# Attention, routed experts and a SoLU layer: another order in attention and at its two ends, and a shorter way to the first expert

## The chip, the cores and the metric

One core of a Trainium2 chip runs the whole program. The time is device microseconds (us) for one execution; smaller is better. Three timed runs of the kernel before gave 783.28, 784.56 and 783.23 us, median 783.28.

## The reference

Three stages in float32, each on the output of the one before.

- Attention in chunks, 4 batches, 8 heads, 768 positions, head size 64. Each chunk of 32 queries sees 8 memory keys, 16 keys to its left, its own 32 and 8 to its right: `a = exp(s - max(s)); a / (sum(a) + 1e-9); out = a @ v`.
- A mixture of experts over 3072 tokens of 512, 8 experts, 1024 hidden. `logits = x @ w_gate`; all 3072 * 8 pairs are taken from the largest logit down, each token goes to the first expert that still has room, and an expert holds 384 tokens. Then `relu(x @ w1[e]) @ w2[e]` for the tokens of expert e.
- A SoLU layer: `h = x @ w_in`, `h * softmax(h)`, a layer norm over 1024 with scale g, and `@ w_out`.

## The kernel before

Two rows and columns of float32r stand for one float32 number: a tile is split in a rounded high part (`..h`, made by ScalarE) and the rest (`..l`, made by VectorE), and a product is three matmuls, high*high, low*high, high*low. So each weight and each activation needs a conversion before TensorE can use it.

**Attention** (`attention`) goes over 24 tiles of 128 queries (NT = 24). Iteration i of one loop works on several tiles: sums(i-1), score(i), less(i) (subtract the maximum), trans(i-2) (transpose the probabilities), expo(i), pv(i-3) (times V), xtrans(i-4) (transpose the result for the gate), and the gate's matmuls every four tiles. Five more iterations drain the pipeline. k is read into block-diagonal tiles KD (5 buffers) and v into VD (4 buffers), whose zeros are set once, by VectorE and GpSimd in turn; the loads of k, q and v are issued on SP's queue, five tiles ahead for k and q. The last four tiles' logits come from `gate_last`, eight matmuls each. The matmul results lie in four kinds of PSUM banks of two buffers each, s, t, o and, for the probabilities' transposes, those of x and the gate's, t again.

**Conversions.** w_in and w_out come as 64-bit numbers. A chunk of 512 columns (`Fixed.chunk`) is loaded on SP's queue, then goes through a step of ScalarE, four of VectorE (in the rows: `e<-v`, `v<-v,e`, `e<-v`, `e<-raw,e`), one of ScalarE and one or two of GpSimd. Seven of w_in's eight chunks are put beside attention, w_out's beside the first two experts.

**The order** of instructions on every engine is written out when the program is built. `Pace` holds a small model of each engine's clock; a generator that says `yield "spare", "dve"` gets its next step only when the model has that engine free before the next due time of more urgent jobs, less a margin `fit` (FIT in the router's first search, and in attention as well, FIT_OUT later). `limit` is the highest rank of job that may go on.

**Routing** (`Route.rounds`): for each expert in turn a search over thresholds (eight comparisons, each counted by TensorE) finds the cut; then prefix sums give each chosen token a slot, and `compact` turns slots into a list of 384 token numbers with one-hot matmuls. It carries a token number as column number and row number in bfloat16, since these keep whole numbers up to 256 only. For expert 0 nothing else can run; from expert 1 on it runs beside TensorE's matmuls.

**Experts** (`Experts.run`): when expert 0 is known its weights are loaded by indirect DMAs on GpSimd's queue, when its tokens are known x is gathered (`gather`), transposed (`x_prep`) and split; then `g12` does the first and second matrix in eight slices, `g3` w_in, `soft` the SoLU, `g4` w_out. `load_w` loads slices of both matrices, `split_w` makes a job that waits for the slice, copies it on ScalarE and subtracts on VectorE.

## Time and profile before

| | |
|---|---|
| median of three runs | 783.28 us |
| profiled execution | 785.33 us |
| its span | 783.6 us |
| TensorE busy (PE) | 715.6 us, 91% |
| VectorE busy (DVE) | 528.2 us, 67% |
| ScalarE busy (ACT) | 335.9 us, 43% |
| GpSimd busy (POOL) | 199.2 us, 25% |
| granted TensorE clock, mean | 0.962 |

The span is the time from the first to the last record; the profiled execution's own time is a little longer. Busy shares are means over stages that differ, so the stages have to be read apart: attention up to about 119 us, the search for expert 0 up to about 145, the first expert up to about 206, and then the stretch in which TensorE hardly stops. Nearly all instructions carry the same line (398), that of the helper which passes them to the model, so groups are told apart by their tiles: `s` scores, `mx` maximum, `p` probabilities, `t` and `pt` their transposes, `o` the product with v, `xs`, `xt` the result and its transposes, `g` the gate, `h` and `y` the first and second matrix of an expert.

### The profile page before, as it was taken

How to read it: one execution, taken by the hardware profiler on the slowest of the kernel's cores; microseconds unless marked ns; L12 is line 12 of the kernel's file. 1: busy time of each engine (PE TensorE's matmuls, PEld its weight loads, DVE VectorE, ACT ScalarE, POOL GpSimd, SP SyncE). 2: the span in 40 equal slices, each digit the busy share in tenths (PEclk: the TensorE clock that was granted, in tenths of full speed). 3: DMA queues.
4: the chain of work that ended last, by engine and by line, in shares of the span. 5: the costliest groups of instructions: out<-in, count | busy, mean ns of one | idle time of the engine just before them, and what ended most of it. 6: DMA issues, size and time to landing. Idle time of an engine off the chain costs nothing.

```text
span 783.6 us, 14636 instructions
## 1 busy us (share of the span) xinstructions
PE 715.6 (91%) x5760; PEld 616.5 (79%) x5760; DVE 528.2 (67%) x1434; ACT 335.9 (43%) x646; POOL 199.2 (25%) x263
## 2 busy tenths in 40 slices
PE   6988784499989999999999999999999999999993
PEld 5766674378869978988898789888988898899882
DVE  7788866589997986972897289639964852553150
ACT  1565550234374354432742273237324632563170
POOL 5234530432441134004101420232023211410121
PEclk8999995689999999999999999999999999999997
DMA  7999873532360044004400430152015110600100
GB/s 252 343 323 331 320 286 132 202 103 60 110 227 1 1 162 131 5 1 147 150 1 17 160 120 1 36 181 81 1 55 188 55 40 28 220 10 1 40 14 27
DMA packets 30020, 89.35 MB, mean 114 GB/s; under 512 B 4224, under 2 KB 4352, under 8 KB 29952
## 3 DMA queue, kind: packets, MB, share of 16 engines
q0 software_dynamic: 13056, 46.14, 17.3%
q1 hardware_dynamic: 16896, 42.28, 15.6%
q8 instruction: 45, 0.74, 0.4%
q14 instruction: 23, 0.19, 0.1%
HBM read 75.83 MB, written 12.58 MB: 113 GB/s over the span
## 4 chain that ended last, share of the span: by engine, by line
PE 72%; DVE 17%; issue 3%; ACT 3%; DMA 2%; POOL 1%; POOLq 0%; DVEq 0%; ACTq 0%
PE h L398 32%; PE y L398 16%; PE o L398 15%; PE tp L398 4%; PE r L398 3%; DVE e L398 3%; DVE sum L398 2%; DMA xg<-x_dram,idx 2%; DVE p L398 2%; DVE mx L398 1%; DVE ge L398 1%; ACT p L398 1%; DVE w1l L398 1%; PE xtp L398 1%; PE g L398 1%
## 5 line engine op out<-in xcount | busy, mean ns | idle before, releaser
L398 PE MATMUL y<-hh,w2h 128*128 128x384 f32 x256 | 91.6, 358 | 7.9 <-DVE e L398 7.9
L398 PE MATMUL y<-hl,w2h 128*128 128x384 f32 x256 | 88.3, 345 | 0.0
L398 PE MATMUL y<-hh,w2l 128*128 128x384 f32 x256 | 87.1, 340 | 0.0
L398 POOL DMA_INDIRECT raw<-in_w_dram,iw x64 | 62.3, 974 | 81.7 <-DVE w1l L398 29.8
L398 POOL DMA_INDIRECT out_dram<-ob,idx x24 | 24.3, 1014 | 227.4 <-ACT ob L398 227.0
L398 DVE TENSOR_REDUCE nm<-h 128x1 f32<-128x512 f32 x48 | 33.0, 687 | 72.6 <-PE h L398 72.3
L398 PE MATMUL o<-out_h,lh 128*128 128x512 f32 x192 | 77.2, 402 | 0.0
L398 PE MATMUL h<-in_h,yh 128*128 128x512 f32 x192 | 76.5, 399 | 0.0
L398 PE MATMUL h<-in_l,yh 128*128 128x512 f32 x192 | 76.2, 397 | 0.0
L398 PE MATMUL h<-in_h,yl 128*128 128x512 f32 x192 | 75.9, 396 | 0.0
L398 PE MATMUL o<-out_h,ll 128*128 128x512 f32 x192 | 75.6, 394 | 0.0
L398 PE MATMUL o<-out_l,lh 128*128 128x512 f32 x192 | 75.1, 391 | 0.0
L398 ACT ACTIVATE hh<-h 128x384 fp32r<-128x384 f32 x64 | 31.4, 491 | 90.4 <-PE h L398 77.3
L398 PE MATMUL h<-xh,w1l 128*128 128x384 f32 x256 | 60.1, 352 | 2.5 <-DVE w1l L398 2.4
L398 PE MATMUL h<-xh,w1h 128*128 128x384 f32 x256 | 59.5, 349 | 1.2 <-ACT w1h L398 1.2
L398 ACT CAST w2h<-raw 128x512 fp32r<-128x512 f32 x64 | 39.6, 620 | 48.0 <-PE y L398 43.5
L398 PE MATMUL h<-xl,w1h 128*128 128x384 f32 x256 | 58.1, 346 | 0.0
L398 PEld LDWEIGHTS y<-hh,w2h 128*128 128x128 f32 x256 | 48.2, 188 | 9.8 <-DVE e L398 9.6
L398 DVE TENSOR_TENSOR xl<-tp,xh 128x512 fp32r<-128x512 f32 x24 | 16.6, 690 | 50.2 <-ACT xh L398 35.2
L398 DVE TENSOR_TENSOR w2l<-raw,w2h 128x512 fp32r<-128x512 f32 x64 | 43.8, 685 | 8.7 <-ACT w2h L398 8.7
L398 PEld LDWEIGHTS h<-xh,w1l 128*128 128x128 f32 x256 | 46.6, 195 | 3.3 <-DVE w1l L398 3.2
L398 PEld LDWEIGHTS y<-hl,w2h 128*128 128x128 f32 x256 | 48.5, 189 | 0.2
(194 smaller groups left out, 1603.1 us busy)
## 6 DMA issues: line engine op xcount, KB each, us to landing
vd<-in_vx_dram SPq DMA_DIRECT2D x48, 256.0 KB, 5.3
kd<-in_kx_dram SPq DMA_DIRECT2D x48, 176.0 KB, 5.0
qt<-in_q_dram SPq DMA_DIRECT2D x24, 256.0 KB, 4.9
x_dram<-xs SPq DMA_DIRECT2D x6, 1024.0 KB, 9.8
raw<-in_win_dram SPq DMA_DIRECT2D x8, 512.0 KB, 6.0
raw<-in_wout_dram SPq DMA_DIRECT2D x8, 512.0 KB, 3.7
raw<-in_w_dram,iw POOLq DMA_INDIRECT x64
xg<-x_dram,idx POOLq DMA_INDIRECT x24
```

What stands on the lines that cost most here:

```text
L398: return fn(*args, **kw)
```

## The change

- Attention: q of a tile is loaded ahead of k. The clears are shared among VectorE, ScalarE and GpSimd in another order. The 20 warm-up transposes go. The router's constants become a job of the model that takes spare steps. In an iteration, score and less come first, then sums of the tile before, then P times V, and only then the exponential; the transposes of the probabilities go to the end. The transposes of x get banks of their own.
- The end of attention: no new conversion steps in the last two tiles and the drain (limit 0); three of the last four tiles' logits go through the short form of the gate, in spare banks of the scores.
- FIT and FIT_OUT are larger.
- Compaction carries a token number as one float16 number between -1536 and 1535; the slot gets 32 added, so that it also says whether a token is chosen.
- First expert: only one slice of w1 is loaded before the gather of x, the others behind it. The first slice is split at once. Small float16 matmuls are issued before and between the transposes of x. The router's round 1 begins when x is ready (`hold`).

```diff
-FIT = 0.34
-FIT_OUT = 0.27
+FIT = 0.62
+FIT_OUT = 0.5
...
 def warm(nc, p, a, n):
     for i in range(n):
-        nc.tensor.transpose(p[:, i % 4], ident, ident)
+        nc.tensor.matmul(p[:, i % 4], a, a, start=True, stop=True)
...
         def load_kq(i):
             if i < NT:
+                nc.sync.dma_start(QT[i % AHEAD], q[i])
                 for h2 in range(2):
                     nc.sync.dma_start(KD[i % AHEAD][h2::2, h2], kx[i, h2])
-                nc.sync.dma_start(QT[i % AHEAD], q[i])
...
-        for i in range(AHEAD):
-            (nc.gpsimd if i % 2 else nc.vector).memset(KD[i], 0.0)
-            if i < AHEAD - 1:
-                (nc.vector if i % 2 else nc.gpsimd).memset(VD[i], 0.0)
+        def clear(t):
+            flat = ...
+            nc.scalar.activation(flat, zero.to_broadcast([128, flat.shape[1]]), AF.Copy)
+        nc.vector.memset(KD[0], 0.0)
+        clear(KD[1])
+        nc.gpsimd.memset(KD[2], 0.0)
+        nc.vector.memset(VD[0], 0.0)
+        clear(KD[3])
+        nc.gpsimd.memset(VD[1], 0.0)
+        clear(VD[2])
+        nc.gpsimd.memset(KD[4], 0.0)
+        nc.gpsimd.memset(VD[3], 0.0)
...
-        consts()
-        warm(nc, ps.tile([128, 4, 128], F32, tag="t", name="warm"), ident, 20)
+        pace.add(consts(), FIRST_C, 0)
...
         for i in range(NT + 5):
+            if i == NT - 2:
+                pace.limit = 0
+            if i < NT:
+                s = score(i)
+                less(i, s)
+                load_kq(i + AHEAD)
             n = 0
             for _ in sums(i - 1) if 0 <= i - 1 < NT else ():
                 beside(i, n)
                 n += 1
-            if i < NT:
-                s = score(i)
-                less(i, s)
-                load_kq(i + AHEAD)
-            if 0 <= i - 2 < NT:
+            if i >= NT and i - 2 < NT:
                 trans(i - 2)
-            if i < NT:
-                expo(i)
             beside(i, 3)
             if 0 <= i - 3 < NT:
                 pv(i - 3)
+            if i < NT:
+                expo(i)
...
-            if i > NT:
-                gate_last(i - 5)
+            if NT < i < NT + 4:
+                gate(NT // 4 - 1, (i - NT - 1,), 2)
+            if i == NT + 4:
+                gate_t(NT // 4 - 1, 3)
+                gate_last(NT - 1)
             if NT + 1 >= i >= 6 and (i - 6) % 4 == 3:
                 gate_t((i - 6) // 4)
+            if 2 <= i < NT:
+                trans(i - 2)
...
-            V.tensor_tensor(slot, slot, sf, op=ALU.mult)
+            V.scalar_tensor_tensor(slot, slot, 32.0, sf, op0=ALU.add, op1=ALU.mult)
             yield 0.0
-            s1 = self.t("s1", [NT])
-            V.tensor_tensor(s1, sel[:, 0], sel[:, 1], op=ALU.add)
...
-        V.scalar_tensor_tensor(am, sl, 32.0, low, op0=ALU.add, op1=ALU.subtract)
-        V.tensor_tensor(am, am, s1, op=ALU.mult)
+        V.tensor_tensor(am, sl, low, op=ALU.subtract)
...
-        V.tensor_tensor(rhs[:, :, 0], rhs[:, :, 1], self.cnum[:, :, None].to_broadcast([128, NT, A]), op=ALU.mult)
-        yield idle
-        V.tensor_scalar(rhs[:, :, 1], rhs[:, :, 1], self.col, None, op0=ALU.mult)
+        V.tensor_tensor(rhs, rhs, self.tok[:, :, None].to_broadcast([128, NT, A]), op=ALU.mult)
...
-        tok = self.t("tok", [TT])
-        V.tensor_scalar(tok, p[:, 0:TT], 128.0, None, op0=ALU.mult)
         idx = self.k.tile([128, TT], I32, name=f"idx{r}")
-        V.tensor_tensor(idx, tok, p[:, TT:2 * TT], op=ALU.add)
+        V.tensor_scalar(idx, p[:, 0:TT], float(N // 2), None, op0=ALU.add)
...
-        self.load_w(0, range(2))
+        self.load_w(0, (0,), (1,))
...
         self.gather(0)
-        self.load_w(0, (2,))
+        self.load_w(0, (0,), (2,))
+        self.load_w(0, (1, 2))
         self.fixed.hold = False
-        for f in range(2):
-            self.split_w(0, f, (1,))
+        self.split_w(0, 0, (1,), True)
+        p = self.ph.tile([128, 4, 128], F32, tag="h", name="warm")
+        warm(nc, p, self.route.ones, 40)
+        for t in range(TT):
+            self.x_prep(0, t)
+            warm(nc, p, self.route.ones, 5)
+        self.split_w(0, 1, (1,))
         for f in range(2):
             self.split_w(0, f, (2,))
-        warm(nc, self.ph.tile([128, 4, 128], F32, tag="h", name="warm"), self.ident, 25)
-        for t in range(TT):
-            self.x_prep(0, t)
         for t in range(TT):
             self.need("x", 0, t)
+        self.route.hold = False
```

## Rows read from the trace of the kernel before

**Rows 1.** Windows: stretch, its length, busy us of each engine, granted clock, DMA share, GB/s.
```profile
12.00:105.00 93.00, 76.62 (x1660) 58.64 (x1664) 74.71 (x150) 52.86 (x101) 39.29 (x34) 0.94 0.90 314
105.00:118.70 13.70, 12.43 (x211) 10.42 (x201) 7.46 (x18) 6.27 (x13) 2.54 (x2) 1.00 1.03 384
...
145.00:153.40 8.40, 5.81 (x38) 4.88 (x36) 1.95 (x4) 2.33 (x5) 4.75 (x5) 0.86 0.84 282
153.40:165.40 12.00, 9.59 (x75) 7.70 (x75) 8.47 (x26) 3.66 (x8) 2.41 (x2) 0.57 0.34 115
165.40:206.00 40.60, 37.99 (x350) 33.44 (x349) 38.95 (x100) 16.31 (x30) 11.06 (x8) 1.00 0.20 58
...
287.00:783.60 496.60, 478.69 (x2710) 419.10 (x2708) 296.28 (x836) 210.89 (x408) 101.58 (x162) 0.99 0.21 70
```

**Rows 2.** Groups of VectorE, 12 to 105 us: count, busy us, mean ns, idle before.
```profile
L398 DVE TENSOR_TENSOR p<-s,mx 128x512 f32<-128x512 f32 x23 | 16.0, 696 | 2.6 <-POOL p L398 0.5
L398 DVE TENSOR_REDUCE sum<-p 128x8 f32<-128x512 f32 x23 | 15.9, 693 | 10.9 <-ACT p L398 10.7
L398 DVE TENSOR_REDUCE mx<-s 128x8 f32<-128x512 f32 x23 | 15.2, 662 | 1.0 <-PE s L398 0.8
L398 DVE TENSOR_SCALAR e<-v 128x512 int32<-128x512 int32 x12 | 8.0, 675 | 0.1
L398 DVE SCALAR_TENSOR_TENSOR v<-v,e 128x512 int32<-128x512 int32 x6 | 5.8, 974 | 0.1
L398 DVE TENSOR_SCALAR sum<-sum 128x8 f32<-128x8 f32 x23 | 5.4, 234 | 0.8
L398 DVE SCALAR_TENSOR_TENSOR e<-raw,e 128x512 f32<-128x512 uint32 x6 | 4.8, 800 | 0.1
L398 DVE RECIPROCAL rec<-sum 128x8 f32<-128x8 f32 x23 | 4.7, 202 | 0.8
```

**Rows 3.** Timeline, attention's first and last maximum: start us, length, engine, what.
```profile
6.78 1.93 PE L398 MATMUL s<-kd,qt 128*32 128x128 f32 x32 [0.88 <-DMA qt<-in_q_dram]
...
9.49 0.13 DVE L398 TENSOR_SCALAR tri<-row,col 128x128 f16<-128x128 bf16 x1
...
11.51 0.06 DVE L398 MEMSET power<- 128x3 f32 x1
...
11.78 0.69 DVE L398 TENSOR_REDUCE mx<-s 128x8 f32<-128x512 f32 x1
...
105.15 0.69 DVE L398 TENSOR_REDUCE mx<-s 128x8 f32<-128x512 f32 x1
```

**Rows 4.** Timeline, TensorE: the scores of two tiles that follow each other.
```profile
21.64 1.05 PE L398 MATMUL s<-kd,qt 128*32 128x128 f32 x32
...
24.80 1.08 PE L398 MATMUL s<-kd,qt 128*32 128x128 f32 x32
```

**Rows 5.** Windows of 2 us in attention's first tiles, for the granted clock.
```profile
18.00:20.00 2.00, 1.88 (x29) 1.39 (x20) 1.42 (x3) 0.56 (x2) 1.04 (x1) 0.50 1.02 381
...
22.00:24.00 2.00, 2.00 (x61) 1.63 (x52) 1.30 (x2) 1.27 (x3) 0.47 (x1) 1.00 1.01 373
```

**Rows 6.** Timeline of the drain: the last tile's probabilities and their product.
```profile
110.66 0.59 ACT L398 COPY pt<-t 128x512 f32<-128x512 f32 x1 [0.35 <-PE t L398]
...
113.48 1.08 PE L398 MATMUL o<-vd,pt 128*32 128x128 f32 x32
```

**Rows 7.** Timeline from expert 0's compaction to its first matmuls.
```profile
141.48 0.29 DVE L398 TENSOR_SCALAR rhs<-rhs,col 128x288 bf16<-128x288 bf16 x1
...
144.68 0.16 DVE L398 TENSOR_SCALAR tok<-r 128x3 f32<-128x3 f32 x1 [0.30 <-PE r L398]
...
145.30 0.95 POOL L398 DMA_INDIRECT xg<-x_dram,idx  x1 [1.78 <-DVE idx L398]
...
149.45 0.66 PE L398 MATMUL tp<-ident,xg 128*128 128x128 f32 x4 [0.58 <-DMA xg<-x_dram,idx]
...
156.81 0.69 PE L398 MATMUL h<-xh,w1l 128*128 128x384 f32 x1 [2.41 <-DVE w1l L398]
```

More of the change, by code (lines that the diff above doesn't have):

```diff
@@ L177, in attention, with spare, gate @@
         G = {}
-        def gate(u, js=range(4)):
+        def spare():
+            return ps.tile([128, 4, 128], F32, tag="s", name="sp")
+        def gate(u, js=range(4), last=3):
             if js[0] == 0:
-                G[u] = ps.tile([128, 128], F32, tag="t", name="g")
+                G[u] = spare()[:, 0] if last < 3 else ps.tile([128, 128], F32, tag="t", name="g")
             for kc in range(4):
@@ L186, in gate @@
                                      skip_group_check=True)
[L187 removed]
+            if js[-1] == last:
+                n = 32 * last + 32
                 g, G[u] = G[u], wk.tile([128, 128], F32, tag="gs", name="gs", bufs=2)
[L189 removed]
+                nc.scalar.copy(G[u][0:n], g[0:n])
         def gate_last(i):
[L193 removed]
+            g = spare()[:, 0, 0:E]
             for kc in range(4):
@@ L531, in __init__ @@
         self.idx, self.iw = {}, {}
-        self.held, self.stage = False, 0
+        self.held, self.stage, self.making, self.hold = False, 0, True, True
     def consts(self, ident):
@@ L750, in rounds @@
             if r:
-                yield from self.compact(r, s1, sl)
+                yield from self.compact(r, sl)
             else:
-                self.beside.add(self.compact(r, s1, sl))
-                while r not in self.idx:
+                self.beside.add(self.compact(r, sl))
+                while r not in self.idx or self.hold:
                     yield 0.0
@@ L862, in load_w, with split_w, parts @@
                 self.W[r, n, qq] = t
-    def split_w(self, r, f, ns=(1, 2)):
+    def split_w(self, r, f, ns=(1, 2), now=False):
         nc = self.nc
-        def parts(n):
+        def parts(n, now=False):
             raw = self.W[r, n, f // 2][:, f % 2]
@@ L870, in parts @@
             lo = self.ws.tile([128, 512], F32R, tag=f"l{n}", name=f"w{n}l")
-            yield raw
+            if not now:
+                yield raw
             nc.scalar.copy(h, raw)
-            yield "act"
+            if not now:
+                yield "act"
             nc.vector.tensor_tensor(lo, raw, h.bitcast(F32), op=ALU.subtract)
@@ L876, in split_w @@
         for n in ns:
-            self.beside.add(parts(n), 0, 0)
+            if now:
+                for _ in parts(n, now):
+                    pass
+            else:
+                self.beside.add(parts(n), 0, 0)
     def gather(self, r):
@@ L1207, in step @@
         beside.tick()
-    attention(nc, tc, q, kx, vx, wg, ident, x_dram, L, lambda: route.consts(ident), step)
+    attention(nc, tc, q, kx, vx, wg, ident, x_dram, L, lambda: route.consts(ident), beside, step)
+    while route.making:
+        beside.tick()
+    beside.limit = 9
     route.open_psum(ctx)
```

63 lines of the change are left out of this document (38 added, 25 removed).

## The prediction

> **What bounds the kernel now.** I read the share of each engine first, then the stretches, then, for each stretch that the change touches, the groups of instructions with the idle time in front of them. The program has two parts. From 287 us on TensorE is busy for 478.69 of 496.60 us at a granted clock of 0.99 [rows 1]: nothing in the change removes TensorE work there, so I count no gain or loss in it. Before that no engine is full, and the time is set by order. In the attention loop (12 to 105 us) VectorE is busy 74.71 us of 93, TensorE 76.62, and the DMA engines 0.90 of the time [rows 1]. The reader is to see in the groups of VectorE that the largest single idle time has one cause: 10.7 us in front of the row sums, released by ScalarE's exponential [rows 2]. The old order issues the exponential of tile i right behind its subtraction and then wants its sum next, so VectorE stands still. A tile takes (105.15 - 11.78) / 23 = 4.06 us [rows 3]. In the drain (105 to 118.7) the engines are a serial chain; the search for expert 0 runs to 145 and is a chain too; then the first expert starts slowly: clock 0.57 from 153.4 to 165.4, and VectorE busy 38.95 of the next 40.60 us [rows 1].
>
> **The sum is made against the profiled execution,** 785.33 us, of which 783.60 are the span and 1.73 lie around it. The median of the three timed runs is 783.28, so 2.05 us come off at the end.
>
> **Attention's start.** Now the scores of tile 0 end at 6.78 + 1.93 = 8.7 us, but their maximum starts at 11.78, since VectorE is first in clears and then, from 9.49 to 11.57, in the router's constants [rows 3]. The change gives VectorE two clears instead of five, moves two to ScalarE (idle then), spreads the constants into later gaps, and sends q, which needs no clear, ahead of k. ScalarE's clears are not in the trace. Below, they cost nothing, as nobody waits for the tiles so early; above, at twice VectorE's time and behind the table load, they would hold k of tile 1 back for about 1 us. I take nothing, as the queue of loads is the slower of the two. If the maximum follows the scores, and these come 0.7 us earlier, it starts at 8.0: -3.8 us, between -2.5 and -4.8.
>
> The 20 warm-up transposes go. Their cover is thin already: with them the granted clock is 0.50 at 18 to 20 us and 1.00 at 22 to 24 [rows 5], so it falls once the first tiles leave TensorE idle and rises again when the tiles follow each other. I take nothing for it. The Trainium skill (TensorE: Matmul & The Clock Gate, "What's actually happening") says that the idle state is the slow one and that activity releases it, which speaks against taking the warm-up out. By that rule the first scores run at 1.2 GHz, one tile's scores take about 2 us and not 1, and the sum would be about 1 us smaller; by the row, the low clock is there anyway and the sum stays.
>
> **The loop.** Per tile VectorE does maximum 0.662, subtraction 0.696, sum 0.693, the small addition 0.234 and the reciprocal 0.202: 2.49 us [rows 2]. Each converted chunk adds two steps of 0.675, one of 0.974 and one of 0.800, 3.12 us, six times in the loop [rows 2]. With 23 tiles that is 57.2 + 18.7, and the wait of 10.7 on top; the rest of the 93 us are small gaps. The new order puts sums(i-1) behind the subtraction of tile i, and the exponential behind P times V, so a sum asks for an exponential that is nearly a whole tile old: the 10.7 us go. The constants come in with 11.57 - 9.49 = 2.1 us. That is -8.6 on VectorE. What is late next? TensorE needs 24.80 - 21.64 = 3.16 us a tile at full clock, before the gate [rows 4], and the DMA share of 0.90 would become 0.90 * 93 / 84.4 = 0.99. Three resources would be full together, so I take 70%: -6.0. The ends: 0 if the stream of inputs holds at its 314 GB/s, -8.6 if nothing else binds; the stream can go faster, as 384 GB/s in the drain shows [rows 1]. Moving the transposes of the probabilities to the end of the iteration takes no instruction away; their reciprocal is a tile old and their bank is no longer shared with the transposes of x, so no wait moves there.
>
> **The drain.** The copy of the last probabilities ends at 111.25, but P times V of that tile starts at 113.48 [rows 6]: TensorE does gate matmuls and waits in between for a bank that VectorE has not freed. The change turns three of four late gates into short ones, with banks of their own, and stops new conversion steps two tiles before the end. I take 2.2 us for that gap, between -1 and -3. The price: about one chunk, 3.1 us of VectorE, is left over for the first expert.
>
> **The search and compaction.** Conversion steps "by room" change only which gap the builder takes. In 118.7 to 145 no step ran before either, so 0; if left-over steps got into the search, 0.7 us each (up to four, +2.8) would be queued ahead of its next comparison. The compaction loses four small VectorE operations for expert 0, of the kind of the row of 0.29 (rhs times column) and the row of 0.16 (tok) [rows 7]: 0.29 + 3 * 0.16 = 0.77, and float16 in place of bfloat16 is the same width: -0.8, between -0.5 and -1.2. For experts 1 to 7 it is hidden by TensorE.
>
> **The first expert.** The gather starts at 145.30, 0.5 us behind the end of tok at 144.84, so GpSimd's queue is not what holds it; its data reach TensorE at 149.45 [rows 7]. Three of the four weight loads ahead of it now come behind it. That is worth 0 (those loads have landed) to -1.5; I take -0.7. The Trainium skill (DMA: Bandwidth & Descriptors, "Anatomy of one DMA") gives 2.0 us plus bytes at 436 GB/s for such a transfer, an estimate of 2.6 us for 0.26 MB against the 4.15 of the row; by it the term would be -1.5. Next, the first weights are split at once, not behind the router's round 1, so the 2.41 us for w1l go [rows 7]. The 55 small warm-up matmuls around the x transposes should keep the clock: 9.59 busy us at 0.57 would take 5.5, -4.1. By the first y matmul that makes -7.2. But it is not kept: VectorE has 1.95 + 8.47 + 38.95 = 49.4 us of work from 145 to 206 [rows 1], plus the left-over 3.1, minus 0.9 for round 1's compaction: 51.6. Begun at the gather's return, 4.4 us in, with 1.6 us of the old gaps, that ends 57.6 us after the token numbers, against 61 now: -3.4. Some steps for w_out may slide behind 206, since they are wanted only at 287; I add 1.1 for them: -4.5, between +1 (the left-over chunk shows in the third matrix) and -9. The held router queues nothing: its work of round 1 began at 153.5 before too. The later weights have cover as well; if it failed, the third slice of w1 would come 1 to 2 us late, inside these ends.
>
> **Sum:** -3.8 - 6.0 - 2.2 - 0.8 - 4.5 = -17.3, so 785.33 - 17.3 = 768.0, and less 2.05, **766.0 us**.
>
> **Rivals.** (a) The stream binds the loop. For it: share 0.90 to 0.99 with both ends measured at 314 and 384 GB/s. Against it: TensorE seldom waits for an input in the loop. The loop gives 0 and the start only the 1.2 us by which the first load is earlier: -1.2 - 2.2 - 0.8 - 4.5 = -8.7, 774.6 us. (b) VectorE gives nothing back in the first expert and the left-over chunk shows: -12.8 + 3.1 = -9.7, 773.6 us. For it: 38.95 busy of 40.60. Against it: w_out's steps can slide. (c) All ends good: -4.8 - 8.6 - 3 - 1.2 - 9 = -26.6, 756.7 us. (d) Slower: without the warm-up TensorE stays at its low clock for many tiles, because at 1.2 GHz the loop is bound by TensorE. The Trainium skill's rule on the idle state (TensorE: Matmul & The Clock Gate, "What's actually happening") would be its ground. A tile then costs 2 * 3.16 + 0.3 = 6.6 and not 3.8, 2.8 us each; from 7 tiles on it eats the 17.3. With ten it is 766 + 28 = 794 us. Against it: a TensorE that is full at the low clock is just what came before the rise between 20 and 22 us [rows 5].
>
> **Chances.** Forecast 0.50 (its own range 760 to 772), (a) 0.22, (b) 0.10, (c) 0.08, (d) 0.08, and 0.02 for a change that does nothing that shows. About 0.2%, 1.6 us, is what a measurement can tell from no change. Faster: the first four less 0.01 of (a)'s edge, 0.89; same 0.03; slower 0.08. The range that holds the time 8 times in 10 is 757 to 779: it takes in (a) and (b) with a bad drain and leaves out (d) and the tail of (c).
>
> **What would show it.** Right: the first maximum near 8 us; no 0.7 us idle in front of the sums, tiles 3.7 to 3.9 us apart; the router's first row at 105 to 109 us, and 25.5 us from there to the token numbers; w1l finished before the first h matmul, and a granted clock near 1.00 through h0 and h1; the first expert's end 56 to 58 us behind the token numbers. Wrong: a DMA share of 1.0 with waits for kd or vd on TensorE (a); TensorE waiting for w1l, w2l or in_l after 150 us (b); a clock of 0.5 beyond 25 us (d); or any change behind 287 us other than a shift.

## The result

In one series the changed kernel took 776.92 us (median of 17 runs) and the kernel before 784.11 us (17 runs): ratio 0.9917, 95% interval 0.9899 to 0.9935, 7.2 us less by the medians where 17.3 were forecast. Two later series with the same kernel gave 0.9978 (0.9959 to 0.9996) and 0.9969 (0.9945 to 0.9993). It is faster, by less than half of the forecast. The 776.9 lies inside the range of 757 to 779, the medians of the two later series (782.92 and 781.26) lie outside it, and the forecast of 766.0 does not hold. One run of each set in the first series, of 1155.85 and 1165.66 us at a low granted clock, is left out of the ratio. The profiled execution has a span of 777.3 us against 783.6.

Where the two profiles part is best read from landmarks, in us from the span's start. A landmark is where the named instruction starts, except for the token numbers, where it is the end; "last split" is the start of the last group of `yl`, the low part of the second matrix's result.

| landmark | before | after | gained in this part |
|---|---|---|---|
| first maximum | 11.78 | 8.60 | 3.2 |
| last maximum | 105.15 | 102.84 | -0.9 |
| router's first row | 118.73 | 118.78 | -2.4 |
| expert 0's token numbers (end) | 145.04 | 143.06 | 2.0 |
| first expert's last split (yl) | 205.30 | 200.83 | 2.5 |
| second expert's | 268.37 | 262.18 | 1.7 |
| last scatter | 772.59 | 766.32 | 0.1 |

Attention, where 12.0 us were forecast, gained nothing in this pair of executions. All that was gained, 6.3 us, lies behind it, where 5.3 (0.8 + 4.5) were forecast.

One profile each is a thin basis, so here are the others, from the experiments below. Six profiles of the changed loop (the changed kernel three times, e3, e12 and e16) have tiles 4.10, 3.97, 3.98, 4.01, 4.01 and 3.94 us apart, two of the old loop (the kernel before and e4) 4.06 and 4.01. By the means, 4.00 against 4.04, the loop's gain is about 0.8 us, with a spread of 0.16 a tile between profiles of one and the same loop. The router's first row comes at 115.84 to 119.25 in five of them (e3 has another drain), at 118.73 and 117.95 under the old attention.

The windows of the kernel after, for the stretches of [rows 1]: length, busy us of TensorE, weight loads, VectorE, ScalarE, GpSimd, then granted clock, DMA share, GB/s.

```profile
12.00:105.00 93.00, 76.90 (x1672) 61.35 (x1663) 76.80 (x165) 53.27 (x101) 40.33 (x43) 0.94 0.92 322
105.00:118.70 13.70, 11.96 (x186) 9.31 (x186) 4.56 (x12) 6.09 (x12) 0.00 (x0) 1.00 1.04 380
145.00:153.40 8.40, 6.02 (x54) 5.20 (x53) 2.39 (x4) 2.79 (x6) 6.27 (x8) 0.86 0.70 218
153.40:165.40 12.00, 10.57 (x89) 8.84 (x88) 8.87 (x26) 4.24 (x9) 5.33 (x5) 0.82 0.76 262
165.40:206.00 40.60, 39.12 (x348) 33.94 (x348) 36.48 (x90) 15.17 (x28) 9.57 (x7) 0.97 0.16 45
287.00:777.30 490.30, 472.97 (x2660) 415.11 (x2660) 288.20 (x797) 205.84 (x399) 100.25 (x161) 0.99 0.20 68
```

The loop's window is nearly the same in every column: the work of 93 us, done in another order. VectorE has 2.1 us more; its conversion steps alone got 2.7 us longer (below). The next fence is the kernel after's groups of VectorE from 12 to 105 us, as in [rows 2].

```profile
L421 DVE TENSOR_TENSOR p<-s,mx 128x512 f32<-128x512 f32 x23 | 16.0, 694 | 2.0
L421 DVE TENSOR_REDUCE sum<-p 128x8 f32<-128x512 f32 x23 | 15.6, 677 | 0.0
L421 DVE TENSOR_REDUCE mx<-s 128x8 f32<-128x512 f32 x22 | 15.1, 685 | 5.2 <-PE s L421 5.0
L421 DVE SCALAR_TENSOR_TENSOR v<-v,e 128x512 int32<-128x512 int32 x6 | 8.5, 1423 | 0.2
```

The wait in front of the sums is gone, as forecast: 10.7 us before [rows 2], 0.0 now. But VectorE's waits, taken together from 8 to 105 us (who waited for whom, total us, times, longest), show where it went. First the kernel before:

```profile
DVE sum L398 <- ACT p L398: 10.7, 16, 0.7
...
DVE mx L398 <- PE s L398: 0.8, 1, 0.8
```

and the kernel after:

```profile
DVE s L421 <- PE s L421: 8.8, 3, 3.9
DVE mx L421 <- PE s L421: 6.1, 5, 2.9
```

Instead of 16 short waits for ScalarE there are 8 long ones for TensorE's scores (`s` is the fill of the edge columns in front of the maximum), of 14.9 us. The first of them, 3.9, stands ahead of the first maximum; the other 11.0 are what the 10.7 became. And TensorE in its turn waits, from 12 to 119 us, for the copies of the transposed probabilities:

```profile
PE o L421 <- ACT pt L421: 10.8, 12, 2.0
PE o L421 <- DMA vd<-in_vx_dram: 3.5, 2, 2.5
```

### The profile page after: what moved, and what is told of

It is laid out like the page before. It is cut to its first block, busy times and chain, and to the rows that moved or that the text cites. A ratio compares the mean times of both kernels' runs of the same rounds, so it can differ in the third digit from the quotient of the medians.

```text
span 777.3 us, 14615 instructions
## 1 busy us (share of the span) xinstructions
PE 710.9 (91%) x5771; PEld 613.4 (79%) x5771; DVE 518.1 (67%) x1398; ACT 341.6 (44%) x650; POOL 199.6 (26%) x263
## 3 DMA queue, kind: packets, MB, share of 16 engines
q1 hardware_dynamic: 16896, 42.28, 15.9%
## 4 chain that ended last, share of the span: by engine, by line
PE 54%; issue 17%; DVE 17%; DMA 5%; ACT 3%; POOL 2%; SPq 0%; POOLq 0%; DVEq 0%
PE h L421 24%; PE o L421 11%; PE y L421 10%; DVE e L421 4%; PE tp L421 3%; PE r L421 2%; DMA xg<-x_dram,idx 2%; DMA vd<-in_vx_dram 2%; DVE p L421 1%; DVE mx L421 1%; DVE v L421 1%; DVE ge L421 1%; DVE sum L421 1%; PE s L421 1%; PE xtp L421 1%
## 5 line engine op out<-in xcount | busy, mean ns | idle before, releaser
L421 PE MATMUL h<-xh,w1l 128*128 128x384 f32 x256 | 58.4, 345 | 0.0
L421 ACT CAST w1h<-raw 128x512 fp32r<-128x512 f32 x64 | 39.6, 619 | 25.6 <-DVE idx L421 25.1
```

What stands on the lines that cost most here:

```text
L421: return fn(*args, **kw)
```

## The experiments

Eighteen kernels ran, in five series (e1 to e4, e5 to e8, e9 to e12, e13 to e15, e16 to e18); every series has the kernel before beside it, at 783.7 to 784.8 us. The series ran on different chips: 0, 3, 15, 0 and 1. A kernel is called by the first part of its name; a piece is one chunk of w_in.

### What holds the loop: four candidates

Four changes of the new kernel, each aimed at one possible link. The first leaves out loads of k, q and v past the first round of buffers, so later tiles compute on old inputs.

```diff
# e1_no_stream, in load_kq (load_v: AHEAD - 1)
-            if i < NT:
+            if i < AHEAD:
# e2_trans_first: ahead of pv(i - 3), no longer at the end of the turn
-            if i >= NT and i - 2 < NT:
+            if 0 <= i - 2 < NT:
                 trans(i - 2)
# e3_one_gate
-            if NT < i < NT + 4:
-                gate(NT // 4 - 1, (i - NT - 1,), 2)
+            if i == NT + 3:
+                gate(NT // 4 - 1, range(3), 2)
# e4_old_attention: attention() of before, all else changed
```

> The changed kernel with the loads of q, k and v left out for all tiles beyond the first ring (five tiles of q and k, four of v); later tiles work on what lies in the buffers, the order of instructions on the engines stays. The attention loop of the changed kernel takes 4.10 us a tile (maxima of tile 0 and 23 at 8.60 and 102.84), no less than before (4.06), and the question is why. Stream theory (the input stream binds the loop): without the stream tiles come 3.6 us apart or less, the last maximum at 92 us or earlier and the router's first row at 108 or earlier. Queue theory (the copy of the transposed probabilities stands behind a younger tile's exponential in ScalarE's queue, that one behind VectorE, and TensorE's P times V waits for it): nothing moves by more than 1 to 2 us, the last maximum at 100 to 103, the router's first row at 116 to 119, and TensorE still waits about 10 us in front of P times V for that copy.

Measured: 777.63 us (one run), the last maximum at 105.76, tiles 4.25 us apart with one conversion more than in the changed kernel. The waits for v are gone and the loop is no faster. The stream of inputs does not bind it; rival (a) falls. TensorE's waits for the copied probabilities, from 12 to 119 us:

```profile
PE o L421 <- ACT pt L421: 18.7, 16, 3.7
```

> The changed kernel with one move: the transposes of the probabilities of tile i-2 (and their copy by ScalarE) stand ahead of P times V and of tile i's exponential, as before the change, and not at the end of the iteration. Everything else is the changed kernel. Queue theory: TensorE's waits for that copy (10.8 us in the loop and drain) go, tiles come 3.6 to 3.8 us apart, the last maximum at 91 to 96, the router's first row at 107 to 112, and the whole takes 766 to 771 us against 777. Stream theory: the loop stays at 4.0 to 4.1 us a tile, the router's first row at 117 to 119, the whole 775 to 778.

Measured: 789.14 us, ratio 1.0073 (1.0051 to 1.0095), tiles 4.55 apart, router's first row at 128.60. The wait for `pt` went, and a larger one for GpSimd's multiplication by the reciprocal came:

```profile
PE t L419 <- POOL p L419: 22.6, 13, 3.9
```

So the new order needs the transposes at the end of the turn: in the old place they ask for probabilities that GpSimd has not yet scaled. Both theories missed; seven pieces were converted here instead of six.

> The changed kernel with the gate's matmuls of tiles 20, 21 and 22 issued together, once tile 22 is there, with a column group of TensorE each, and not tile by tile. In the changed kernel each of the three takes 1.06 us, as much as the eight matmuls (0.96 us) that they replaced. If the drain is bound by TensorE's work: from the last maximum (102.84) to the router's first row (118.78) 13.8 to 14.3 us and not 15.9, the whole 774 to 775.5. If the drain is a chain of copies between engines: 15.5 to 16, the whole unchanged at 777.

Measured: 776.17 us, ratio 0.9879 (0.9846 to 0.9911), not clear of the changed kernel's. From last maximum to router's row 16.8 us instead of 15.9, which looks like the chain of copies. But in this profile TensorE stands still for 2.28 us in the middle of a product with v, with no releaser in the trace ("issue"):

```profile
111.33 0.42 PE L421 MATMUL o<-vd,pt 128*32 128x128 f32 x6 [2.28 <-issue]
```

The changed drain takes 15.9 to 16.0 us where this wait is missing (the changed kernel's first and third profile, e1, e2), and 18.3 and 18.4 where it lasts 2.0 us at a clock of 1.00 (e12, e16). Profiles with the wait have to be compared with each other. From last maximum to router's row, first e3 and then e16:

```profile
100.84:117.60 16.76, 12.37 (x226) 9.47 (x225) 6.63 (x15) 7.24 (x14) 2.18 (x2) 1.00 1.03 378
```

```profile
98.80:117.15 18.35, 14.35 (x226) 11.00 (x224) 6.63 (x16) 7.23 (x14) 2.18 (x2) 1.00 0.99 358
```

One gate group for three takes 2.0 us off TensorE's work and 1.6 us off the drain, near the 1.6 to 2.1 that the first theory forecast. So these profiles speak for a drain that is bound by TensorE's work; in the total it does not show.

> The changed kernel with attention as it was before (order, start and end, the warm-up transposes, the constants all at once); compaction, the margins and the first expert stay changed. If attention's change is worth nothing, as the two traces say (the router's first row at 118.73 and 118.78): router's first row at 118.7, the whole 776 to 778, the same as the changed kernel. If the new attention costs or gives something that shows only later (what is converted by its end): the whole 2 us or more away from 777, below it if the chunk left over by the new end is paid for in the first expert.

Measured: 780.95 us, ratio 0.9961 (0.9944 to 0.9978), router's row at 117.95, 0.8 us ahead of the changed kernel's. The old attention is no slower up to the router. The total is another matter: it lies 4.8 us above e3 in the same series, with intervals that do not meet, so the second branch came, and the new attention gave something that shows only later. In the profiles it shows in the second expert: its last split starts at 262.87 against 260.51 in e3, while the first expert's starts at 198.92 and 199.25. TensorE waits there 2.3 us for the conversion step `e`, as it does for 2.9 in the kernel before and not in e3 or the changed kernel. Why is open, and in the last two series, with another wait in the first expert (below), the changed kernel is no faster than e4 was.

### The exponential last

```diff
-            if i < NT:
-                expo(i)
...
                 trans(i - 2)
+            if i < NT:
+                expo(i)
```

> The changed kernel with the exponential of a tile issued at the end of the turn, behind the copy of the transposed weights of the tile two earlier, so that this copy no longer stands behind an exponential that waits for VectorE. Queue theory (ScalarE's order binds the loop): TensorE's waits for the copied weights (10.8 us in the changed kernel between 12 and 119) go to under 3 us, tiles come 3.5 to 3.7 us apart instead of 4.1, the router's first row is at 107 to 112 instead of 118.8, and the whole takes 766 to 771 us. Conversion theory (the conversion steps hold the loop up wherever they stand in VectorE's and GpSimd's queues): another wait takes the place, tiles stay at 4.0 or more, the router's first row is at 117 or later, 775 to 785 us.

Measured: 779.1 us, ratio 0.9942 (0.992 to 0.9963); tiles 4.00 apart, router's row at 118.57. TensorE's waits from 12 to 119 us:

```profile
PE t L421 <- POOL p L421: 6.4, 7, 1.9
PE s L421 <- issue: 4.0, 3, 1.8
PE o L421 <- DMA vd<-in_vx_dram: 3.5, 4, 1.3
PE t L421 <- DVE p L421: 2.6, 1, 2.6
PE o L421 <- ACT pt L421: 2.2, 3, 1.0
```

The 10.8 us for `pt` fell to 2.2 as the queue theory had it, and nothing was gained: other links took the place, and the wait for v stayed at 3.5. The theory that ScalarE's order binds the loop fell here; tiles, row and total are what the conversion theory forecast.

### Attention without conversions, in both orders

```diff
-CHUNKS_A = 7
+CHUNKS_A = 0
```

> The changed kernel with no conversion of the first expert's weights beside attention: all eight pieces are converted later, in front of the first expert, so only attention's own part of the run is read. Conversion theory: tiles come 3.2 to 3.5 us apart instead of 4.1 and the last maximum is near 84 to 90. Queue theory alone: tiles stay at 3.9 or more.

> The kernel before with no conversion beside attention in the same way. If the order of work is worth something of itself, its tiles come 0.3 us or more further apart than those of the changed kernel without conversions (the forecast's loop gain); if the old wait of the sums for the exponential was only the place where VectorE stood idle for another's sake, the two orders run within 0.1 us a tile of each other.

Measured (totals of 812.11 and 803.97 us mean nothing here, since eight conversions came later). New order: maxima from 8.66 to 91.38, (91.38 - 8.66) / 23 = 3.60 us a tile. Old order: 11.78 to 92.02, 3.49 us. The forecast's 0.3 us a tile would have shown; **the new order shows no gain of its own** (the 0.1 that it is slower lies inside the spread between profiles). The granted clock is not the reason: from tile 4 on, when it is 1.00 in both loops up to the last maximum, tiles come 3.68 (new) and 3.56 us (old) apart. Without conversions the old order still shows its wait for the exponential, 13.9 us, and the new order has none. VectorE's groups from 12 to 105 us, first the old order, then the new:

```profile
L398 DVE TENSOR_REDUCE sum<-p 128x8 f32<-128x512 f32 x24 | 16.6, 692 | 13.9 <-ACT p L398 13.9
L398 DVE TENSOR_REDUCE mx<-s 128x8 f32<-128x512 f32 x24 | 15.9, 663 | 1.5 <-PE s L398 1.2
```

```profile
L421 DVE TENSOR_REDUCE sum<-p 128x8 f32<-128x512 f32 x24 | 16.3, 680 | 0.0
...
L421 DVE TENSOR_REDUCE mx<-s 128x8 f32<-128x512 f32 x22 | 15.2, 691 | 14.5 <-PE s L421 14.2
```

13.9 us in front of the sums became 14.2 in front of the maxima. Here VectorE is not the bound; the window of 12 to 105 us of the old order says what is:

```profile
12.00:105.00 93.00, 87.14 (x1860) 68.45 (x1860) 61.66 (x139) 52.02 (x99) 22.94 (x22) 1.00 0.95 327
```

TensorE is busy 87.14 of 93 us, and VectorE's idle time was slack beside it. In the new order it is busy 81.60: it waits itself, 3.5 us for `pt` and 3.2 for v. With conversions TensorE is not full in either order (76.62 and 76.90 of 93), so what holds that loop is not shown by this pair. What a conversion costs the loop is: (4.10 - 3.60) * 23 / 6 = 1.9 us in the new order (1.3 with the 3.94 of e16) and (4.06 - 3.49) * 23 / 6 = 2.2 in the old, against 3.12 us of VectorE for one [rows 2].

### What of a conversion costs the loop

```diff
 e8_no_pool_conv
-            G.tensor_tensor(v if wide else lo, v, hi.bitcast(F32), op=ALU.subtract)
-            if wide:
-                G.tensor_tensor(lo, v, e, op=ALU.add)
+            G.memset(lo.bitcast(F32), 0.0)
 e11_half_steps
+            B = C if m else C // 2
+            for b in range(0, C, B):
+                yield "spare", "dve"
+                V.tensor_scalar(ei[:, b:b + B], vi[:, b:b + B], ...)     # so for each step
```

> The changed kernel with GpSimd's two steps of each conversion replaced by one fill of the low part with zero, so the low part of the weights is left out of the result. If the conversions hold the loop up by the time GpSimd and VectorE take together (contention theory), VectorE's first rounding step falls from 1.42 us to about 0.7 and tiles come 3.6 to 3.8 us apart; if it is ScalarE's queue, the tiles stay at 4.0 or more.

Measured: 773.85 us (one run), tiles 3.83 apart, router's row at 114.01. The tiles were right and the way was not: VectorE's `v<-v,e` still took 1.43 us, so it is not slowed by the conversion's own GpSimd steps. What it stands beside is GpSimd's scaling of the probabilities. In the kernel before, the step of one conversion, behind the end of a scaling (52.46):

```profile
52.88 0.68 DVE L398 SCALAR_TENSOR_TENSOR v<-v,e 128x512 int32<-128x512 int32 x1
```

and in the kernel after, a scaling on GpSimd and the step beside it:

```profile
45.91 1.12 POOL L421 TENSOR_TENSOR p<-p,rec 128x512 f32<-128x512 f32 x1 [0.43 <-DVE L L421]
```

```profile
46.17 1.41 DVE L421 SCALAR_TENSOR_TENSOR v<-v,e 128x512 int32<-128x512 int32 x1
```

All six such steps of the changed loop, and of e8, lie beside a scaling and take 1.41 to 1.44 us. Of the six in the kernel before, four have GpSimd idle and take 0.68 to 0.69, two lie beside its work and take 1.65 and 1.43; 974 and 1423 ns are means of such mixtures. So the new order, which starts conversions right behind the reciprocal that releases GpSimd, pays (1.423 - 0.974) * 6 = 2.7 us of VectorE that the forecast did not have.

What the loop gains in e8 must come through GpSimd's queue, where the scaling stands behind the conversion's steps; that is argued, not shown. GpSimd's share is (4.10 - 3.83) * 23 / 6 = 1.0 us of the 1.9 that a conversion costs, or 0.4 with the 3.94 of e16.

> The changed kernel with each VectorE and GpSimd step of w_in's conversion cut in two halves of 256 columns, each placed by itself: the same work in smaller pieces, plus about 6 x 0.06 us a piece of weights for the further instructions. Theory of blocking (a step that stands in front of a tile's link is too long): tiles 3.7 to 3.9 apart, the router's first row at 111 to 115, 769 to 773 us. Theory of amount (VectorE and GpSimd together take so much of the loop however it is cut): tiles 4.1 to 4.2, the row at 118 to 121, 776 to 780 us.

Measured: 802.82 us, ratio 1.0214 (1.016 to 1.0268). Only five pieces were converted beside attention; tiles 3.97 apart, router's row at 120.00. Each piece cost (3.97 - 3.60) * 23 / 5 = 1.7 us, inside the 1.3 to 1.9 of whole steps, so no gain from smaller steps shows. Neither theory has the total: three pieces were left over instead of two, and TensorE waits once for 10.5 us for `out_h`, the converted w_out. That the third piece brought it is argued, not shown.

### The drain

```diff
+            if i >= NT - 1:
+                add_up()          # sums(i - 1), ahead of score(i) in the last turn
             if i < NT:
                 s = score(i)
                 less(i, s)
...
-            if i >= NT and i - 2 < NT:
+            if i >= NT - 1 and i - 2 < NT:
                 trans(i - 2)
...
-            if NT < i < NT + 4:
-                gate(NT // 4 - 1, (i - NT - 1,), 2)
-            if i == NT + 4:
-                gate_t(NT // 4 - 1, 3)
-                gate_last(NT - 1)
+            if i > NT:
+                gate_last(i - 5)
```

> The changed kernel with the sums of tile 22 put back ahead of the scores of tile 23, the transposition of tile 21 ahead of P.V of tile 20 in that turn, and a gate matmul group of eight for each of the last four tiles as in the kernel before; the loop up to tile 22 is the changed one. Theory A (the drain is longer because tile 22's weights wait behind the scores of tile 23, and one more P.V stands behind the last maximum): from the last maximum to the router's first row 13.5 to 14.5 us instead of 15.9, the row at 115.5 to 117.5, 773.5 to 776 us. Rival (the drain is bound by the last tile's own chain, or the last maximum moves by as much): the row stays at 118 to 119.

Measured: from last maximum (101.72) to the router's row (114.04) 12.3 us instead of 15.9, the row 4.7 us ahead of the changed kernel's first profile. Theory A holds for the drain, and more strongly than expected; the edit changes three things at once (the sums, the transposes, the gates), so their shares are not told apart. The rows of the kernel after show the largest. VectorE and TensorE at the end of its loop:

```profile
102.84 0.69 DVE L421 TENSOR_REDUCE mx<-s 128x8 f32<-128x512 f32 x1
103.63 0.69 DVE L421 TENSOR_TENSOR p<-s,mx 128x512 f32<-128x512 f32 x1
104.24 0.68 DVE L421 TENSOR_REDUCE sum<-p 128x8 f32<-128x512 f32 x1
...
105.40 0.69 DVE L421 TENSOR_TENSOR p<-p,rec 128x512 f32<-128x512 f32 x1
```

```profile
104.12 0.60 PE L421 MATMUL t<-ident,p 128*128 128x128 f32 x4
106.24 0.63 PE L421 MATMUL t<-ident,p 128*128 128x128 f32 x4 [1.51 <-DVE p L421]
...
111.58 1.06 PE L421 MATMUL sp<-xt,wg 128*32 128x128 f32 x8
...
114.43 1.06 PE L421 MATMUL sp<-xt,wg 128*32 128x128 f32 x8
```

The sum at 104.24 is tile 22's, and it stands behind the last tile's maximum and subtraction. Its scaled probabilities are there at 106.1, so TensorE stands idle for 1.51 us and starts that tile's transposes 3.4 us behind the last maximum; with the old last turn they start 0.3 us behind it:

```profile
101.72 0.69 DVE L424 TENSOR_REDUCE mx<-s 128x8 f32<-128x512 f32 x1
```

```profile
102.01 0.60 PE L424 MATMUL t<-ident,p 128*128 128x128 f32 x4
```

The pipeline is one step deeper, and the whole tail of products and gates comes behind that step. Behind the last maximum TensorE is busy 12.28 of 13.58 us in the kernel before, 13.84 of 15.94 in the changed one and 11.64 of 12.32 in e10: the drain is nearly full of its work, and the change put more of it there. The short gates (`sp`) take 1.06 us each, where the old ones of eight matmuls take 0.96, here in the old order without conversions:

```profile
98.88 0.96 PE L398 MATMUL g<-wg,xt 128*128 128x8 f32 x8
```

In total this kernel took 780.41 us, ratio 0.9953 (0.9928 to 0.9978), so the 4.7 us did not arrive, and theory A's total is missed; a wait with no releaser stands in the first expert of this profile (below). Run again beside the changed kernel:

> The changed loop with the old last turn, a second time, in one series with the changed kernel. If the shorter drain is a gain that lasts: 2 to 5 us below the plain repeat. If it is given back in front of the first expert's end whatever the stall does: within 1 us of the repeat.

Measured: 780.94 us, ratio 0.9961 (0.9945 to 0.9976), last maximum 101.66, row at 113.99, as the first time. The changed kernel in that series took 781.26, and its own row came at 115.84 in its profile: 1.9 us lay between the two at the row, 0.9 at the last scatter, 0.3 between the medians. The shorter drain is there in both profiles, but the total does not show it. Where the last 0.9 us went is open.

### The start, under the old order

```diff
 e9_old_order_new_start: loop and drain in the order of before; start, compaction, first expert changed
 e13_old_order_34: the same, attention's fit 0.34 again, no "pace.limit = 0"
 e14_drain_seven: e10_old_drain without
-            if i == NT - 2:
-                pace.limit = 0
```

> The changed kernel with the order of the loop and the drain of the kernel before; of the change's attention only the start stays (queries loaded first, clearing by three engines, constants made in the loop's room, no warm-up). Theory A (the new order gains nothing in the loop and its last turn is longer, the start is a gain of its own): first maximum near 8.5, tiles 4.05 apart, drain 13.5 to 14, the router's first row at 115 to 116.5 instead of 118.8, 772 to 775 us. Theory B (the conversions, spaced out by the builder's model, set the end of the loop, and an earlier start is waited out in it): last maximum at 104 or later, the router's first row at 117.5 to 119, 776 to 779 us.

Measured: 801.31 us. Its first maximum is at 8.06 and its router's row at 106.51, but only two pieces were converted beside attention: under the old order the model finds so little spare room that the constants, which rank ahead of conversions, were made until 82 us. Neither theory had that.

> The order of the loop and of the drain of the kernel before with the changed start, compaction and first expert; the room asked for a step beside attention is 0.34 again and conversions go on in the drain. (In the run of the old order with 0.62 the making of the constants lasted until 82 us and held the conversions back, so only two pieces were converted beside attention; this run is to have seven.) If the start is a gain of its own: first maximum near 8.1, router's first row at 114.5 to 116, seven pieces, 772 to 776 us. If an earlier start is waited out in the loop or taken by the constants: the row at 117 to 119, 777 to 781 us.

Measured: 796.36 us, ratio 1.016 (1.0144 to 1.0175); row at 106.00, three pieces converted, the constants made until 71 us. Missed again, for the same reason. With e7 (start at 11.78, no piece, row at 105.60) it fits a start that is worth its 3.7 us in the old order if a piece costs 1.4; that is not a test, and the point stays open. Five and six pieces left over, in these two kernels, go with totals of 796 and 801 us.

> The kernel with the changed loop and the old last turn, with conversions allowed in the drain, so that the seventh piece of w_in is converted beside attention as in the kernel before instead of behind the first expert's weights. If a late piece has a price of some 3 us (the changed kernel left two pieces where the one before left one): the row at 114 to 116, one piece left over, 771 to 775 us. If pieces converted beside the first expert cost nothing: 776 to 780 us, as the run with six.

Measured: 784.94 us, ratio 1.0009 (0.9996 to 1.0023). Seven pieces, one left over, as before the change; but the row came 5.7 us later (119.71 instead of 114.04) and the rest of the kernel was no shorter. The profile also has the longest waits of the next section, so the price of a late piece is not read from it alone; nothing speaks for the 3 us.

### The first expert, and the same kernel three times

> The changed kernel with the first expert's opening as before: both pieces of weights loaded ahead of the gather, all four splits ahead of x's preparation, 25 transpositions as warm-up, and the router's next round not held back. If the order there is what shortened the first expert: its first result ends 60 us or more behind the token numbers instead of 57.8, and the whole takes 779 to 782 us. If the shortening came from elsewhere (GpSimd's and ScalarE's queues being empty, the router): 57.8 stays, 776 to 778 us.

With the old opening (loads of two slices ahead of the gather, all splits ahead of x, 25 transposes as warm-up): 785.18 us, ratio 1.0015 (0.9993 to 1.0037); the first expert's last split starts 61.2 us behind the token numbers instead of 57.8, and TensorE waits for w1l again (2.0 us). So the opening is a gain, and without it nothing is left of the whole change.

> The changed kernel once more, to stand beside the other two in the same series. 775 to 778 us by all theories; the other two beat it only if their intervals lie below its own.

Measured: 782.92 us (12 runs), 6 us more than in its first series. ScalarE from the gather on, first in the first profile of the changed kernel, then in this one:

```profile
148.44 0.59 ACT L421 CAST xh<-tp 128x512 fp32r<-128x512 f32 x1 [4.75 <-PE tp L421]
149.72 0.59 ACT L421 CAST xh<-tp 128x512 fp32r<-128x512 f32 x1 [0.69 <-PE tp L421]
151.78 0.59 ACT L421 CAST xh<-tp 128x512 fp32r<-128x512 f32 x1 [1.47 <-PE tp L421]
```

```profile
148.62 0.59 ACT L421 CAST xh<-tp 128x512 fp32r<-128x512 f32 x1 [4.33 <-PE tp L421]
152.92 0.59 ACT L421 CAST xh<-tp 128x512 fp32r<-128x512 f32 x1 [3.71 <-remote]
155.82 0.59 ACT L421 CAST xh<-tp 128x512 fp32r<-128x512 f32 x1 [2.31 <-PE warm L421]
```

The second rounding of x waited 3.71 us for something that no engine in the profile released ("remote"), and TensorE 4.16 us in front of the third transposes ("issue"). The first matmul of h came 13.0 us behind the token numbers instead of 9.4. Such a wait, of 1.9 to 6.5 us and several times 3.7, stands in all six profiles of the third and fourth series that have the new opening, and in none of the first two series. The chip alone does not decide it: chip 0 ran the first series of experiments without it and the fourth series with it.

```diff
 e16_hold_weights
-        self.load_w(0, (0,), (2,))
-        self.load_w(0, (1, 2))
...
             self.x_prep(0, t)
             warm(nc, p, self.route.ones, 5)
+            if t == 1:
+                nc.gpsimd.memset(held[:, 0:1], 0.0)    # held: the second piece of x
+                self.load_w(0, (0,), (2,))
+                self.load_w(0, (1, 2))
```

> The changed kernel a third time. If its time is set by whether the stall of ScalarE in the first expert is there: 776 to 778 us without the stall, 781 to 784 us with it. If the difference between its first two series had another cause, the profile shows a stall with the low time or none with the high one.

> The changed kernel with the first expert's later weight loads held on GpSimd until TensorE has transposed the second piece of x (a one-column fill of that piece stands in front of them). In the repeat of the changed kernel ScalarE stood 3.7 us at the second rounding of x with no releaser in the profile and TensorE 4.2 us at the third transposition, while the weights' loads kept the DMA engines 0.9 busy; the first run of the same kernel had neither. Theory of contention (the stall comes from what the weights' loads displace): the stall is gone, the first matmul of h comes 9 to 10 us behind the token numbers, and the kernel is 2 to 4 us faster than the plain repeat in this series. Rival (the stall has another cause, or is not there in this series): no stall to remove or it stays, and the later weights cost 0 to 2 us against the plain repeat.

Measured: the changed kernel 781.26 us, with two such waits (6.0 us together) in its profile and h 12.9 us behind the token numbers; the kernel that holds the weight loads 782.14, with none, and h 9.1 us behind. So the wait is missing where the loads are held, which speaks for contention, but one profile each is no proof; e18 in the same series has the wait. In total nothing was won: TensorE's waits for the router's `ge` (7.2 us from 150 to 300, 1.3 in the changed kernel) took the place. That the wait sets which of its two times the changed kernel takes agrees with its three series, but is not shown: e16 has none and takes as long. What brings it to some series and not to others stays open. The router's row of the changed attention came at 118.78, 119.25, 115.84 and 117.15 in these profiles.

## Why the prediction was wrong

**The step that failed is the loop's**: "the 10.7 us go ... That is -8.6 on VectorE", of which 70% were taken as time of the loop. The first half came out: no wait is left in front of the sums. The second treated idle time of an engine that is busy 80% of the loop as time of the loop. Of the -6.0 us the first pair shows +0.9, and all profiles together about -0.8. The pair without conversions shows that there the wait was slack beside TensorE; with conversions its removal moved it to the maxima, 11.0 us for 10.7. The question "what is late next?" was answered with shares of busy time (TensorE 3.16 us a tile, the DMA share), and these left room; it was not asked what VectorE would find when it arrived earlier. It found scores that were not ready. A second term was put at nothing: the conversion's step kept its 0.974 us in the sum, and took 1.423 beside GpSimd's scaling, 2.7 us in the loop.

**The drain** (-2.2) was +2.4 in the first pair. Its reading was wrong: the gap in [rows 6] was taken for a wait. Of its 2.23 us TensorE waits 0.26 in the kernel before; the rest are transposes of x, a gate and that gate's transpose, the last of which is this row:

```profile
113.22 0.33 PE L398 MATMUL g<-ident,gs 128*128 128x128 f32 x1 [0.26 <-DVE L L398]
```

So the gap is still there in the changed kernel (the copy of the last `pt` ends at 110.74, its product starts at 112.83), and the short gates are not short. And a cost was missed: sums(i-1) behind less(i) is paid once at the end; with the old last turn and the old gates the drain is 3.6 us shorter (e10). The diff shows that plainly: whatever a turn does later, the last turn does later too.

**The start** (-3.8) measured -3.0 to -3.7 at the first maximum, and was lost by the loop and the drain in the first pair. ScalarE got three clears and not two (the diff has KD[1], KD[3] and VD[2]); they took 1.3 to 1.9 us each, about as long as VectorE's. Rival (d) did not come: at 18 to 24 us the granted clock is 1.00 in the changed kernel, where it was 0.50 up to 20 us [rows 5]:

```profile
18.00:20.00 2.00, 1.97 (x48) 1.53 (x52) 1.93 (x4) 0.83 (x2) 1.04 (x1) 1.00 0.97 342
...
22.00:24.00 2.00, 2.00 (x50) 1.63 (x43) 1.86 (x7) 1.16 (x3) 0.45 (x1) 1.00 0.93 312
```

That is one profile: with the same start the clock is 0.60 and 0.50 at 15 to 18 us in e16 and e18. And the row of the clock, 1.00 from the first window on, does not tell all. The first tiles' scores take as long in the changed kernel as under a granted 0.50 in the kernel before (1.94 us at 17.36), and those from 19.70 on do not:

```profile
6.36 1.94 PE L421 MATMUL s<-kd,qt 128*32 128x128 f32 x32 [6.36 <-DMA kd<-in_kx_dram]
...
19.70 1.08 PE L421 MATMUL s<-kd,qt 128*32 128x128 f32 x32
```

By the Trainium skill's rule (TensorE: Matmul & The Clock Gate, "What's actually happening") a loss of 1 us had been priced. The trace agrees with its size: the first tile's scores took 1.94 us, and 1.93 with the warm-up too [rows 3], but those of the second and third took 1.94 each, and 1.75 and 1.08 with the warm-up. Over the first five tiles the scores take 1.1 us more. Whether the loop is longer by it is not shown; the forecast had put this term at nothing.

**Search and compaction** (-0.8) gave 2.0, of which the removed operations are the forecast part. The rest is a wait of VectorE for the first one-hot counts that fell from 1.49 to 0.37 us. It is not the compaction's doing, for the old compaction shows 0.39 in e7 and the new one 1.32 in e12. So the 2.0 is in part luck.

**The first expert** (-4.5) gave -2.5 at its last split and -4.2 one expert later. Its end lay 57.8 us behind the token numbers, against 60.3 before; the 57.6 that were worked out had been measured to a mark 0.7 us later. The wait for w1l is gone, and TensorE's clock from 153.4 to 165.4 was 0.82 instead of 0.57, not the 1.00 that was asked for: it held 1.00 up to 160 us and was 0.50 from 162 to 166. The gather was no faster: its first piece of x reaches TensorE 3.9 us after its issue begins, 4.15 before [rows 7], and 4.7 us behind the token numbers against 4.4 before, where -0.7 had been taken. So the estimate of 2.6 us from the Trainium skill (DMA: Bandwidth & Descriptors, "Anatomy of one DMA") does not hold here; the profile's own median from issue to landing is 3.5 us.

Rival (a) had the nearest number, 774.6, with a mechanism that e1 refutes: that nearness is luck. Rival (b) did not come: one piece more was left over, as the forecast itself had it, but VectorE did give time back.

## What to carry to other kernels

Before idle time of one engine is counted as a gain, take out the competing work and run both orders: if they take the same time, the wait is slack, and removing it only moves it. Work that is put a step later in a software pipeline is paid once more in the drain. And time and profile the same kernel in more than one series: the first gave 0.8%, the second and third 0.2 and 0.3%, and one profile with a wait of 2 us that another lacks turned the reading of e3 round.

## What the hardware showed

- A wait of 1.9 to 6.5 us with no releaser in the profile, of ScalarE and with it TensorE and VectorE, in some series of the same program. A transfer of 0.02 MB on the queue named "instruction" falls into the stretch behind the gather, in profiles with and without the wait.
- A wait of TensorE of 2.0 to 2.3 us with no releaser in the drain, each time behind 26 of the 32 matmuls of the same product with v (e3, e12, e15, e16), and missing in other profiles of the same order (the changed kernel's first and third). From 104 to 114 us each of the four has a transfer on the queue named "instruction" and the changed kernel's first profile has none; its third has one without the wait, so the cause is open.
- Eight matmuls of a gate with 32 columns each took 1.06 us (`sp`), 32 such matmuls for four tiles at once 1.08 us: four column groups together cost what one costs.
- VectorE's integer step `v<-v,e` of 128 x 512 took 0.68 to 0.69 us where GpSimd stood idle and 1.41 to 1.65 where GpSimd worked beside it, in the kernel before, the changed kernel and e8.
